# Which engine copies the transposed q and k out of PSUM in three slots of a fused attention and feed-forward kernel, and where two split products close

## The chip, the cores and the metric

The kernel runs on one core of a Trainium2 chip. A core has engines that run side by side and meet through semaphores: TensorE (matrix products and transposes, PE in the profile), VectorE (DVE), ScalarE (ACT), GpSimd (POOL) and SyncE (SP, which here only issues DMAs). Each engine takes its instructions in the order in which they were written. The metric is the device time in microseconds: a median of 348.01 us over 3 runs (348.01 to 348.04).

## The reference

Batch 8, 8 heads, sequence 576, head dimension 64; then a feed-forward layer over 4608 tokens of width 512, with 2048 hidden units.

```python
scores = scale * np.matmul(q, k.transpose(0, 1, 3, 2))
cum = np.cumsum(np.log(np.clip(f, 0.0001, 1.0)), axis=-1)
decay = cum[:, :, :, None] - cum[:, :, None, :]
scores = np.where(causal, -1000000000.0, scores + decay)
attn = np.exp(scores - np.max(scores, axis=-1, keepdims=True))
attn = attn / (np.sum(attn, axis=-1, keepdims=True) + 1e-09)
x = np.matmul(attn, v)            # heads side by side: (4608, 512)
h = x @ w_in                      # (4608, 2048)
out = (h - np.tanh(h)) @ w_out    # (4608, 512)
```

## The kernel before

Work is dealt in **slots** `p`, one for each pair of heads: slot p is batch p // 4, pair p % 4, so there are 32, and one more at the end. `NPAIR` is 4. Slot p computes the scores of its pair, the attention values of the pair before (`values`), and, early in the program, transposes q and k of a pair that comes next. Between these, a loop deals steps of the feed-forward layer, in order, so many to a slot (`TAKE`: 2 in slot 4, 7 in slot 5, 6 in each of slots 6, 7 and 8, 8 in slot 9).

**Scores.** A slot has seven tiles (`TILES`), each of up to 512 columns in one PSUM bank: `scores` (L306) issues the products K^T Q on TensorE (L326), an exp on ScalarE (L335), and, from batch 1 on, the causal mask on GpSimd (L345). The score banks are two (`ps_sc`), taken in turn, so a tile's products wait until the exp of the tile two before has read its bank. Tile 3 is the small one that both heads share.

**Transposes.** `trans` (L254) does a pair of heads' q or k for the first three batches: six transposes on TensorE (L264) into one PSUM bank, then two copies into `QT` or `KT`, one for the even and one for the odd positions (64x576 each). The letters of `copies` say which engine makes each copy: "V" is VectorE (L277), "A" is ScalarE (L275). From slot 4 on, the bank is the single one of the pool `ps_tr`. So the transposes of k wait until both copies of q have read that bank, and the next q for both copies of k. From batch 3 on, q and k are transposed by DMA and `trans` isn't used.

**Where they stand.** `att_items` (L547) writes a slot's list of items. In slots 4 to 6 the next pair's q is transposed at tile 0 and its k at tile 2 (slot 4) or 3 (slots 5, 6), with "VV". Slots 7 and 8 do two pairs of batch 2 each: q at tiles 0 and 4, k at tiles 2 and 6, with "VA" for both. There the copy on ScalarE waits for the one on VectorE.

**The feed-forward steps.** `mlp1(u, ft)` (L398) makes one 128x512 tile of h from four chunks of input (`XR`, one chunk for each pair of heads; L408), a tanh on ScalarE (L413) and an add on VectorE into `gq` (L417). Its PSUM bank comes from the three of `ps_m`, in turn; the tanh's tile `th` has two buffers. `mlp2_plain` (L436) makes a fourth of an output tile (L442) from `gq`; every fourth step ends with a copy on ScalarE (L446) and a DMA out. Slots 4 and 5 and most of slot 6 deal `mlp1` steps; slots 7 and 8 deal `mlp2_plain` steps only. The first two `mlp1` tiles are split in slot 4: three chunks first (part 0), and the last chunk with tanh and add later (part 1), since that chunk comes from the pair of the slot before, transposed and copied into `XR` by ScalarE (L378) in the same slot.

**Order.** Everything is under a manual schedule: each engine executes in the order in which the program emits. An item that counts (`put`) may be followed by a feed-forward step; one that doesn't (`items.append((fn, False))`) never moves them. The subtractions on the second layer's weights (L245) stand as such items at tiles 1, 3 and 5 of slots 7 and 8.

Of the kernel before, what the change touches and what calls it, by code (L numbers as in the profile page):

```python
# [21 lines left out]
def kernel(  # L22
# [18 lines left out]
    NPAIR = H // 2  # L41
# [39 lines left out]
    qn, kn = ([t[0:S // NT6, :].rearrange("p (h n d) -> p h n d", h=H, n=NT6) for t in raw] for raw in (qraw, kraw))  # L81
    qb, kb = ([t[:, 0:NJ * DM].rearrange("p (n e) -> p n e", n=NJ) for t in raw] for raw in (qraw, kraw))
    vn = [qkp.tile([P, NJ, H, VW], FP16, tag=f"vn{i}", name=f"vn{i}") for i in range(2)]
    QT = [qkp.tile([D + 3, H, S], FP16, tag=f"QT{i}", name=f"QT{i}") for i in range(2)]
    KT = [qkp.tile([D + 3, H, PITCH], FP16, tag=f"KT{i}", name=f"KT{i}") for i in range(2)]
# [82 lines left out]
    def load_aug(b):  # L168
        i, hs = b % 2, slice(b * H, (b + 1) * H)
        eng = nc.gpsimd if b == 0 else nc.sync  # L170
        eng.dma_start(out=KT[i][D:D + 1, :, 0:S], in_=chi[hs, :])
        eng.dma_start(out=QT[i][D + 2:D + 3, :, :], in_=cq[hs, :])
        eng.dma_start(out=KT[i][D + 1:D + 2, :, 0:S], in_=clo[hs, :])

    def const_rows(i):
        nc.sync.dma_start(out=QT[i][D:D + 2, :, :], in_=minus16)
        nc.sync.dma_start(out=KT[i][D + 2:D + 3, :, 0:S], in_=ones16[0:H, :])
# [76 lines left out]
    def trans(b, c, src, dst, early, copies, split=False):  # L254
        pn, g3 = S // NT6, NT6 // 2
        if early:
            t32 = ps_m.tile([P, UW], FP32, tag="m", name="t32")
            t16 = t32.bitcast(FP16)[:, 0:2 * S // 2].rearrange("p (a g n) -> p a g n", a=2, g=g3)
        else:
            t32 = ps_tr.tile([P, UW], FP32, tag="tr", name="t32")  # L260
            t16 = t32.bitcast(FP16)[:, 0:2 * S // 2].rearrange("p (a g n) -> p a g n", a=2, g=g3)
        for a in range(2):
            for g in range(g3):
                nc.tensor.transpose(out=t16[:, a, g, :],  # L264
                                    in_=src[b % 2][:, 2 * c + a, 2 * g:2 * g + 2, :],
                                    identity=id16[0:pn, 0:pn])
        parts = [(a, e) for a in range(2) for e in range(2)] if split else [(slice(0, 2), e) for e in range(2)]

        def copy(a, e, eng):
            if split:  # L270
                a = slice(a, a + 1)
            to = dst[b % 2][0:D, 2 * c:2 * c + 2, e:S:2].rearrange("d a (p g) -> d a p g", g=g3)[:, a]
            of = t16[e * D:(e + 1) * D, :, :, :].rearrange("d a g p -> d a p g")[:, a]
            if eng == "A":
                nc.scalar.activation(out=to, in_=of, func=AF.Copy)  # L275
            else:
                nc.vector.tensor_copy(out=to, in_=of)  # L277

        todo = [lambda a=a, e=e, eng=eng: copy(a, e, eng) for (a, e), eng in zip(parts, copies)]
        for fn in todo[:2]:  # L280
            fn()
        return todo[2:]

    def head_tiles(a):
        return [[(a, 0, 0, 512, 0)],
                [(a, 1, P, 448, 0), (a, 0, 512, 64, 448)],
                [(a, 2, 2 * P, 320, 0), (a, 3, 3 * P, 192, 320)]]

    TILES = head_tiles(0) + [[(0, 4, 512, 64, 64), (1, 4, 512, 64, 128)]] + head_tiles(1)
    LAST = 3  # L290
    MASKS = {0: (0, 1, 1, P), 1: (0, 1, 1, P), 2: (0, 2, 320, P), 3: (64, 2, 64, 64),
# [229 lines left out]
    def start():  # L521
        unread(33)
        q_rest = trans(*pairs[0], qn, QT, True, "AAAA", True)
        nc.scalar.activation(out=cq, in_=cum, func=AF.Copy, bias=-SHIFT * inv_qscale, scale=inv_qscale)
        nc.scalar.activation(out=expo, in_=lf[0:1, 0:1], func=AF.Exp)
        unread(6)
        k_rest = trans(*pairs[0], kn, KT, True, "VVVV", True)
        unread(22)
        decay(0)
        unread(8)  # L530
        scores(*pairs[0], 0)
        for fn in k_rest:
            fn()
        q_rest[0]()
        scores(*pairs[0], 1)
        q_rest[1]()
        for e in EL[0:2]:
            nc.vector.memset(e, 0.0)
        nc.vector.memset(KT[0][:, :, S:PITCH], 0.0)
# [7 lines left out]
    def att_items(p):  # L547
        def put(fn, *args):
            items.append((lambda: fn(*args), True))

        items = []
        here = pairs[p] if p < len(pairs) else None
        before = pairs[p - 1] if 0 < p <= len(pairs) else None
        after = pairs[p + 1] if p + 1 < len(pairs) else None
        early = p < NPAIR
        for ti in range(len(TILES)):
            if here and (p > 0 or ti > 1):
                put(scores, *here, ti)
            if p == 1 and ti == 6:
                items.append((lambda: const_rows(1), False))  # L560
                items.append((lambda: load_aug(1), False))
            if early and p > 0 and ti in (0, 6):
                put(unread, 2)
            if p == 1 and ti == 3:
                put(last)
            for load in LOADS.get((p, ti), ()):
                items.append((load, False))
            at_q, at_k = (1, 3) if p == 0 else (0, 1) if early else (0, 2) if p == NPAIR else (0, 3)
            if p in (2 * NPAIR - 1, 2 * NPAIR) and ti % 2 == 0:
                pair = pairs[2 * NPAIR + 2 * (p - 2 * NPAIR + 1) + ti // 4]  # L570
                put(trans, *pair, *((kn, KT) if ti % 4 else (qn, QT)), False, "VA")
            if ti == at_q and p < 2 * NPAIR - 1:
                put(trans, *after, qn, QT, early, "VV")
            if p == NPAIR:
                if ti in (3, 4):
                    put(mlp1, 0, ti - 3, 1)
            if ti == at_k and p < 2 * NPAIR - 1:
                put(trans, *after, kn, KT, early, "VV")
            if p == NPAIR:
                if ti == 1:  # L580
                    put(turn, *pairs[p - 2])
                    put(values, *before)
                    put(mlp1, 0, 0, 0)
                elif ti == 2:
                    put(mlp1, 0, 1, 0)
                    put(turn, *before)
            elif early and ti in (2, 3) and before:
                put(values, *before, (ti - 2,))
            elif not early and ti == 2 and before:
                put(values, *before)  # L590
            if p < NPAIR:
                if ti == 1 and p > 1:
                    put(turn, *pairs[p - 2])
            elif p > NPAIR and ti == 3:
                put(turn, *before)
        return items
# [9 lines left out]
    with tc.manual_schedule(engines=FIVE):  # L606
        bulk()
        for p in range(len(pairs) + 1):
            b, c = divmod(p, NPAIR)
            items = att_items(p)  # L610
            take = TAKE[p] if p < len(TAKE) else 8 - (p - len(TAKE)) % 2
            if p == 2 * NPAIR + 1:
                widen(1)
            mine = mlp[at:at + take]
            at += take
            first = 14 if p == NPAIR else 0
            if p == len(pairs):
                for fn, *args in mine[0:2]:
                    fn(*args)
                mine = mine[2:]  # L620
            given, n = 0, 0
            whole = sum(counts for _, counts in items)
            for emit, counts in items:
                emit()
                n += counts
                while n > first and given < len(mine) and given * (whole - first) < (n - first) * len(mine):
                    fn, *args = mine[given]
                    fn(*args)
                    given += 1
        widen(2)  # L630
        for fn, *args in mlp[at:]:
            fn(*args)
# [28 lines left out]
```

## Time and profile before

| | |
|---|---|
| median of 3 runs | 348.01 us |
| the profiled execution's own time | 347.95 us |
| its span | 346.2 us |
| VectorE copies of q and k, 64x576 | 0.80 us each |
| ScalarE copies of q and k, 64x576 | 0.81 us each |
| ScalarE exp of 128x512 | 0.60 us each |

The page gives busy time, share and number of instructions for each engine; a stretch gives its length, then each engine's busy time, the granted TensorE clock, the DMA engines' share and what they moved. A timeline line gives start, length, engine, line, operation and, in brackets, how long the engine had been idle and who ended that. A line of the waits gives who waited for whom, the sum, how often and the longest. TensorE's products overlap: a 128x512 product is shown 0.38 us long, but four of them take 0.86 us.

### The profile page before, as it was taken

Reading aid. Unit: us, or ns where it says so; the run is one execution under the profiler, and the core shown is the slowest. Engines: PE = TensorE matmul, PEld = TensorE weight load, DVE = VectorE, ACT = ScalarE, POOL = GpSimd, SP = SyncE. Lnnn points to the kernel's source line nnn. Section 1 sums busy time; section 2 is a strip of 40 time slices with the busy share of each in tenths; the row PEclk is TensorE's granted clock in tenths of the full one; section 3 lists DMA queues with packets and bytes.
Section 4 is the critical chain, followed back from the end, with each engine's and each line's share of the span. In section 5 each row is a group of like instructions: output and inputs, shape, how many; then the busy total and the mean of one; then the engine's idle time right before and its main releaser. Section 6 shows DMA issues by size and latency. Waiting matters only on the chain.

```text
span 346.2 us, 8606 instructions
## 1 busy us (share of the span) xinstructions
PE 335.2 (97%) x3253; PEld 230.6 (67%) x3253; DVE 261.7 (76%) x504; ACT 232.6 (67%) x437; POOL 161.3 (47%) x319
## 2 busy tenths in 40 slices
PE   8988998889999999999999999999999999999995
PEld 7476554555578656865688888755875587487485
DVE  6599787564988788678867886788677766876874
ACT  5687886777897787778767876788548842632640
POOL 8974652676558655765577465742322210000000
PEclk9999999999999999999999999999999999999999
DMA  8999999999999999799979997991131013003003
GB/s 108 147 182 201 193 201 154 107 114 177 132 130 105 177 137 122 94 176 137 117 78 200 130 128 78 186 143 27 49 97 31 17 50 110 0 14 109 0 11 113
DMA packets 144877, 38.80 MB, mean 112 GB/s; under 512 B 128148, under 2 KB 143236, under 8 KB 144836
## 3 DMA queue, kind: packets, MB, share of 16 engines
q0 software_dynamic: 92480, 18.39, 69.7%
q1 hardware_dynamic: 52356, 19.88, 30.5%
q8 instruction: 25, 0.41, 0.5%
q14 instruction: 16, 0.13, 0.1%
HBM read 36.85 MB, written 9.44 MB: 134 GB/s over the span
## 4 chain that ended last, share of the span: by engine, by line
PE 87%; DVE 6%; ACT 4%; issue 1%; DMA 1%; ACTq 0%
PE hps L408 32%; PE ops L466 28%; PE ps L326 12%; PE av L357 8%; PE ops L442 3%; DVE gq L417 2%; ACT e L335 2%; DVE QT L277 2%; PE t L264 1%; DVE KT L277 1%; PE ps L329 1%; DMA TQ<-in_f_dram 1%; PE ps L297 1%; ACT QT L275 1%; ACT th L413 1%
## 5 line engine op out<-in xcount | busy, mean ns | idle before, releaser
L408 PE MATMUL hps<-XR,win 128*128 128x512 f16 (+1 forms) x640 | 140.9, 357 | 0.9 <-ACT XR L378 0.7
L413 ACT ACTIVATE th<-hps 128x512 f32<-128x512 f32 x144 | 86.9, 603 | 55.4 <-PE hps L408 54.6
L335 ACT ACTIVATE e<-ps 128x512 f16<-128x512 f32 x192 | 110.5, 598 | 14.1 <-PE ps L326 6.0
L417 DVE TENSOR_TENSOR gq<-hps,th 128x512 f16<-128x512 f32 x144 | 98.4, 688 | 26.0 <-ACT th L413 24.6
L345 POOL TENSOR_SCALAR_AFFINE_SELECT e<-e 128x128 f16<-128x128 f16 x168 | 60.4, 361 | 78.0 <-ACT e L335 76.1
L408 PEld LDWEIGHTS <-win 128*128 128x128 f16 x640 | 57.7, 97 | 48.4 <-issue 0.5
L326 PE MATMUL ps<-QT,KT 67*128 67x64 f16 (+5 forms) x384 | 77.9, 276 | 3.1 <-ACT e L335 1.7
L466 PEld LDWEIGHTS <-gq 128*128 128x128 f16 x640 | 60.4, 97 | 11.1
L466 PE MATMUL ops<-wout,gq 128*128 128x256 f16 x512 | 63.2, 272 | 0.0
L326 PEld LDWEIGHTS <-KT 67*128 67x128 f16 (+1 forms) x384 | 36.7, 98 | 25.5 <-DVE KT L277 1.6
L357 PEld LDWEIGHTS <-e 128*128 128x128 f16 x896 | 32.2, 97 | 3.9
L357 PE MATMUL av<-vn,e 128*128 128x65 f16 x896 | 33.6, 193 | 0.0
L119 POOL DMA_DIRECT2D vn<-in_v_dram x32 | 28.0, 878 | 8.7 <-DMA win<-in_moe_w_in_dram 4.1
L466 PE MATMUL ops<-W,sq 128*128 128x256 f16 x256 | 31.2, 272 | 0.0
L366 DVE TENSOR_TENSOR xn<-av,rs 128x640 f16<-128x640 f32 x32 | 26.4, 825 | 1.1
L466 PEld LDWEIGHTS <-sq 128*128 128x128 f16 x256 | 24.2, 98 | 3.4
L96 POOL DMA_DIRECT2D kn<-in_k_dram x25 | 21.2, 848 | 1.5 <-issue 1.3
L345 POOL TENSOR_SCALAR_AFFINE_SELECT el<-el 128x128 f16<-128x128 f16 x28 | 9.4, 334 | 26.9 <-ACT el L335 26.2
L96 POOL DMA_DIRECT2D qn<-in_q_dram x25 | 21.2, 848 | 1.3 <-issue 0.8
L364 DVE TENSOR_SCALAR rs<-av 128x10 f32<-128x10 f32 x32 | 5.2, 162 | 19.0 <-PE av L357 17.9
L277 DVE COPY QT<-t 64x576 f16<-64x576 f16 x18 | 14.5, 803 | 6.2 <-PE t L264 6.1
L277 DVE COPY KT<-t 64x576 f16<-64x576 f16 (+1 forms) x22 | 16.3, 739 | 3.8 <-PE t L264 3.6
(82 smaller groups left out, 307.5 us busy)
## 6 DMA issues: line engine op xcount, KB each, us to landing
out_dram<-ost SPq DMA_DIRECT2D x34, 256.0 KB
vn<-in_v_dram POOLq DMA_DIRECT2D x24, 128.0 KB, 5.6
qn<-in_q_dram POOLq DMA_DIRECT2D x20, 128.0 KB, 4.3
kn<-in_k_dram POOLq DMA_DIRECT2D x20, 128.0 KB, 4.6
win<-in_moe_w_in_dram POOLq DMA_DIRECT2D x2, 1024.0 KB, 14.8
wout<-in_moe_w_out_dram POOLq DMA_DIRECT2D x2, 1024.0 KB, 14.1
XR<-xn SPq DMA_TRANSPOSE x56
vn<-in_v_dram POOLq DMA_DIRECT2D x12, 64.0 KB, 5.2
```

Source lines behind the costliest of these rows:

```text
L96: nc.gpsimd.dma_start(out=dst[b % 2][0:pn, n, :].rearrange("p (h d) -> p h d", h=H), in_=src[b, :, n * P:n * P + pn, :].rearrange("h p d - ...
L119: nc.gpsimd.dma_start(out=vn[b % 2][:, n, h0:h1, 0:D], in_=v[b, h0:h1, n * P:(n + 1) * P, :].rearrange("h p d -> p h d"))
L277: nc.vector.tensor_copy(out=to, in_=of)
L326: nc.tensor.matmul(out=ps[:, col:col + n], lhsT=KT[b % 2][0:rows, h, j * P:(j + 1) * P], rhs=QT[b % 2][0:rows, h, i0:i0 + n], start=not ow ...
L335: nc.scalar.activation(out=e[:, lo:hi], in_=ps[:, lo:hi], func=AF.Exp, scale=qscale)
L345: nc.gpsimd.affine_select(out=view, in_=view, compare_op=ALU.is_ge, fill=0.0, base=0, pattern=pat, channel_multiplier=-1)
L357: nc.tensor.matmul(out=av[:, a, ib, :], lhsT=E.pop((b, c, a, j, ib)), rhs=vn[b % 2][:, j, 2 * c + a, 0:D + 1], start=(j == 0), stop=(j == ib))
L366: nc.vector.tensor_tensor(out=xn.rearrange("p i (a d) -> p a i d", a=2), in0=av[:, :, :, 0:D], in1=rs.to_broadcast([P, 2, NJ, D]), op=ALU. ...
L408: nc.tensor.matmul(out=hps[:, o:o + n], lhsT=win[:, ci, ft * P:(ft + 1) * P], rhs=XR[:, ci, t:t + n], start=(ci == 0), stop=(ci == NCH - 1))
L413: nc.scalar.activation(out=th, in_=hps, func=AF.Tanh, scale=-1.0)
L417: nc.vector.tensor_tensor(out=GQ[(u, i)][:, half, kt, :], in0=hps, in1=th, op=ALU.add)
L466: nc.tensor.matmul(out=ps[:, m, :], lhsT=LHS[lhs](u, kt // 4)[:, kt % 4, m * P:(m + 1) * P], rhs=rhs[:, kt, :], start=(fresh and (apart or ...
```

## The change

In slot 6, q's two copies move from VectorE to ScalarE ("AA"); k's stay on VectorE. In slots 7 and 8, q's two copies are both ScalarE's and k's are both VectorE's ("VV"). With "AA" only the first copy is emitted right behind the transposes; the second is kept in a list and emitted at the next tile, behind that tile's exp. In slot 4 the second parts of the two split first products stand at tiles 4 and 5 instead of 3 and 4.

```diff
@@ trans @@
-        for fn in todo[:2]:
+        now = 1 if copies == "AA" else 2
+        for fn in todo[:now]:
             fn()
-        return todo[2:]
+        if copies == "AA":
+            LATER.extend(todo[now:])
+        return todo[now:]
...
+    LATER = []
+
+    def rest():
+        LATER.pop()()
@@ att_items @@
             if p in (2 * NPAIR - 1, 2 * NPAIR) and ti % 2 == 0:
                 pair = pairs[2 * NPAIR + 2 * (p - 2 * NPAIR + 1) + ti // 4]
-                put(trans, *pair, *((kn, KT) if ti % 4 else (qn, QT)), False, "VA")
+                put(trans, *pair, *((kn, KT, False, "VV") if ti % 4 else (qn, QT, False, "AA")))
+            elif p in (2 * NPAIR - 1, 2 * NPAIR) and ti % 4 == 1 or p == 2 * NPAIR - 2 and ti == 1:
+                items.append((rest, False))
             if ti == at_q and p < 2 * NPAIR - 1:
-                put(trans, *after, qn, QT, early, "VV")
+                put(trans, *after, qn, QT, early, "AA" if p == 2 * NPAIR - 2 else "VV")
             if p == NPAIR:
-                if ti in (3, 4):
-                    put(mlp1, 0, ti - 3, 1)
+                if ti in (4, 5):
+                    put(mlp1, 0, ti - 4, 1)
```

## The prediction

> **What bounds the kernel now.** I read the page's engine shares and slices first, then the busy times by stretch, the waits, the chain of waits over 53 to 68 us, and the timelines of ScalarE and TensorE through slots 4 to 9. Slots are told in the trace by their first score product, 512 columns wide. I write sc0 to sc6 for a slot's seven score tiles, M1, M2, ... for the feed-forward steps dealt between them, Q and K for six transposes of q or k.
>
> The page's engine line, and the stretches of slot 6, slot 7, slot 8 and the start of slot 9:
>
> ```profile
> PE 335.2 (97%) x3253; PEld 230.6 (67%) x3253; DVE 261.7 (76%) x504; ACT 232.6 (67%) x437; POOL 161.3 (47%) x319
> 47.50:56.60 9.10, 7.98 (x78) 4.45 (x78) 8.04 (x14) 7.18 (x14) 3.11 (x10) 1.00 1.66 186
> 56.60:66.60 10.00, 8.96 (x90) 5.19 (x91) 6.12 (x11) 6.13 (x11) 5.69 (x11) 1.00 1.63 115
> 66.60:77.10 10.50, 9.14 (x91) 5.20 (x91) 6.18 (x11) 8.01 (x14) 6.66 (x12) 1.00 1.19 109
> 77.10:90.00 12.90, 12.90 (x106) 6.88 (x106) 7.81 (x14) 10.78 (x21) 8.17 (x17) 1.00 1.65 169
> ```
>
> TensorE is the first figure after the stretch's length: full from 77.1 us on (its waits there sum to 0.2), about 1 us short in each of slots 6, 7 and 8. So whatever moves sc0 of slot 9 (77.09) moves the end one for one, at a granted clock of 1.00. The chain of waits in slots 6 and 7 shows the shortfalls:
>
> ```profile
> 55.71 0.81 DVE KT L277
> 56.52 0.05 issue
> 56.57 0.39 PE ps L326
> ...
> 57.83 0.27 PE t L264 x6
> 58.10 0.02 issue
> 58.12 0.81 DVE QT L277
> 58.93 0.02 issue
> 58.95 0.82 ACT QT L275
> 59.77 0.04 issue
> 59.82 0.41 PE t L264 x6
> ```
>
> First, slot 7's sc0 waits for slot 6's last k copy on VectorE. Then K waits for both q copies, because Q and K share one PSUM bank: Q starts at 57.66, K at 59.82, 2.16 us, with the ScalarE copy strictly behind the VectorE one. The other three gaps from Q to K are 63.85 to 66.00, 68.14 to 70.29 and 74.32 to 76.47, 2.15 each. ScalarE's own order and durations (start, length):
>
> ```profile
> 47.56 0.60 ACT L413 ACTIVATE th<-hps 128x512 f32<-128x512 f32 x1 [0.67 <-DVE gq L417]
> 48.05 1.08 ACT L335 ACTIVATE e<-ps 128x512 f16<-128x512 f32 x2
> 49.01 1.29 ACT L413 ACTIVATE th<-hps 128x512 f32<-128x512 f32 x2
> 50.20 1.08 ACT L335 ACTIVATE e<-ps 128x512 f16<-128x512 f32 x2
> 51.15 0.62 ACT L413 ACTIVATE th<-hps 128x512 f32<-128x512 f32 x1
> ...
> 58.95 0.81 ACT L275 ACTIVATE QT<-t 64x576 f16<-64x576 f16 x1 [1.29 <-DVE QT L277]
> 59.79 1.09 ACT L335 ACTIVATE e<-ps 128x512 f16<-128x512 f32 x2
> ```
>
> An exp or tanh is 0.60 long, but the next starts 0.48 after it (they overlap by 0.12); a 64x576 copy is 0.81 and the next starts 0.83 to 0.84 after it (seven cases in slots 7 and 8). The same copy on VectorE is 0.80, a pair 1.60. For slot 4, three lines of the waits:
>
> ```profile
> PE t L264 <- ACT QT L275: 1.7, 4, 0.4
> PE hps L408 <- ACT XR L378: 0.7, 1, 0.7
> PE ps L326 <- ACT e L335: 0.4, 2, 0.2
> ```
>
> **Slot 4.** Removed nothing; the fourth input chunk of M(0,0) and M(0,1), with their tanh and VectorE add, goes behind one more score tile. No DMA is issued by these steps and none is passed on SP or POOL. Now TensorE stands from 34.25 to 34.93 for the ScalarE copy into XR, with sc4 behind it, and ScalarE idles 0.30 (35.05 to 35.34) before the first tanh. After it, sc4 (0.22, its bank free at 34.00) runs in that hold and its exp takes the idle time. ScalarE then runs at its 0.48 pitch from 35.03; the first tanh comes at 35.51 instead of 35.34, but the fourth at 37.91 instead of 38.23. VectorE's add of slot 5's M1, where the chain moves onto VectorE, was at 39.89 and comes at about 39.65, since M1's last product ends 38.97. From there VectorE is on the chain up to 47.46, and hands the gain to the tanh at 47.56: -0.24. Bounds: -0.30 (all of the idle time); +0.20 if the later first add keeps M(0,3) waiting for its bank, by the one such wait shown (TensorE on the add, 0.20). If that cover failed, VectorE would start its q pair in slot 5 later.
>
> **Slot 6.** VectorE loses the q pair (50.27 to 51.90, 1.63). ScalarE gains two copies: the first behind M1's tanh, the second behind sc1's exp, so both stand ahead of M3's tanh. ScalarE's queue is in order, and from 47.56 it was nearly full: tanh, exp, exp, tanh 49.01, copy 49.50, tanh 50.33, exp 50.81, copy 51.31, exp 52.14, tanh of M3 52.62 to 53.22 (it was 51.15 to 51.77). Who waits: M3's add on VectorE, and behind it in VectorE's queue the division of the attention values, M4's add and the k pair. Before, add 52.54, first division step 53.13, k pair 54.92 to 56.52. After, the add starts 53.27, the division 53.87 (0.60 on, as in the trace), the k pair 55.66 (1.79 on), and ends 57.26; sc0 of slot 7 at 57.31 instead of 56.57: +0.74. VectorE's saved 1.63 turns into idle time before its adds. The q pair itself is done at 52.12, ahead of K at 52.63. Bounds: +0.98 if a copy doesn't overlap the exp or tanh ahead of it (the start-up copies of q show a step of 0.50 after the exp at 9.72 and 0.62 after that at 10.75; I take 0.50, as between the exp at 68.11 and the output copy at 68.61), and -1.26 if the relief arrived whole: sc6 leaves TensorE at 55.31.
>
> **Slots 7 and 8.** Each Q to K gap was 0.46 (transposes to first copy), 0.83, 0.82, 0.05. Now the two copies are on ScalarE with sc1's (or sc5's) exp between: 0.46 + 0.83 + 0.50 + 0.81 + 0.05 = 2.65, +0.49 or so each. Work between Q and K on TensorE is 1.57, so all of it is stall. In slot 8's second gap M5's output copy (0.60, started 0.20 after Q at 74.52, pitch 0.50) is ahead of the first copy: 0.70 + 2.19 = 2.87 instead of 2.15, +0.72; before, VectorE's half hid it. K to the next Q: k pair 0.46 + 1.61 + 0.05 = 2.12 against 2.14 where it bound (66.00 to 68.14): nothing; from slot 7's and slot 8's first K to Q2 TensorE's own 4.03 covers it. The division behind the k pair starts 2.2 after K, the pair ends 2.07 after it: covered by 0.1. The exp of sc5 no longer follows both copies, so sc0 of slot 9 doesn't wait for it: K to sc0 was 0.62 (76.47 to 77.09), becomes the transposes' 0.26: -0.36. The same wait at slot 8's start gives nothing, since Q behind it waits for the k pair anyway. Sum 3 x 0.49 + 0.72 - 0.36 = +1.83. Bounds: +2.31 with 0.12 more at each exp-to-copy step; +1.35 if the four first copies overlapped their exps by 0.12 as exps do; as a floor -0.72, both sc0 waits and nothing else. I take the rows of these very copies.
>
> The Trainium skill (ScalarE: Activation LUTs, What ACT_TABLE_LOAD costs) says that back-to-back ACTIVATEs overlap by about 93 ns. By it the six copies followed by an exp or tanh would cost 0.56 less, and the time would be about 349.7; the trace agrees for exps (0.12) and not for these copies.
>
> **Sum.** -0.24 + 0.74 + 1.83 = +2.33 against the profiled execution's 347.95 us (span 346.2), which is 0.06 under the median of 348.01: 350.3.
>
> **Rivals.** A, not slower: VectorE's relief reaches slot 7. The place is M3's tanh in slot 6. Ending at 51.77 as now, it would let the add start at 51.82 and the k pair end at 55.81: sc0 at 55.86, -0.71, total +0.88, 348.8; earlier still, sc0 comes at 55.31, -1.26, total -0.24 - 1.26 + 1.83 = +0.33, 348.3. It decides where that tanh ends before about 51.6 instead of 53.22: then slot 6's term is -0.87 and the sum within 0.70. For it: VectorE is the fullest engine there after TensorE (8.04 of 9.10). Against: two copies, 1.67 us, ahead of a tanh that had 0.77 of slack (its end at 51.77, its add at 52.54). B, not slower: sc1's exp doesn't separate the halves, both run back to back before it. Then the gaps are 0.46 + 0.83 + 0.81 + 0.05 = 2.15 as now, 0.20 more for the output copy, and -0.24 + 0.74 + 0.20 - 0.36 = +0.34, 348.4. For it: nothing but that order; against: in this trace every engine follows the order written. A with B: -1.66, 346.3. C, slower still: the copies don't overlap what is ahead of them: -0.24 + 0.98 + 2.31 = +3.05, 351.0, and with slot 4 at its +0.20, +3.49, 351.5. For it: the step of 0.62 at start-up; against: the 0.50 there and after other exps.
>
> **Numbers.** About 0.2% (0.70 us) is what a measurement of this kernel can tell from no change. Forecast 0.74, with its own range 349.5 (-0.30 + 0.50 + 1.35) to 351.0; C 0.10; A 0.08; B 0.04; A with B 0.04. Slower 0.84, same 0.12, faster 0.04. Low 348.9, part way to A, since slot 6 may give back some; high 351.5 from C.
>
> **What would show it.** Right: the gap from Q to K near 2.65 three times and 2.87 once; M3's tanh in slot 6 later by over 1 us and sc0 of slot 7 waiting for KT near 57.1; sc0 of slot 9 near 79.4; TensorE full after it. Slot 4: no hold for XR with sc4 behind it, and slot 5's first add 0.2 earlier. Wrong: a KT ready before slot 6's last score tile; K starting 2.2 after Q; ScalarE copies shorter than 0.8; or idle time after slot 9 that takes up the delay.

## The result, and the profile after

The changed kernel takes 350.04 us (median of 5, 350.02 to 350.9) against 348.03 (348.01 to 348.07): 2.01 us slower; over all five runs the ratio is 1.0064, 95% interval 1.0052 to 1.0075. Some runs show a granted clock of 0.993 to 0.995 and take 0.7 to 1.7 us longer (two of these five, seven of the 12 of slot 6 alone and two of the six with q in another bank, both below), and no difference told here rests on them. The forecast was 350.3, slower, in a range from 348.9 to 351.5.

The page's engine line after, and the stretches of slot 6, slot 7, slot 8 and the start of slot 9, whose bounds have moved with the slots (length, then TensorE, its weight loads, VectorE, ScalarE, GpSimd, the granted clock, DMA share, GB/s):

```profile
PE 334.9 (96%) x3253; PEld 230.0 (66%) x3253; DVE 260.2 (75%) x502; ACT 234.1 (67%) x439; POOL 162.3 (47%) x319
47.20:57.00 9.80, 8.05 (x79) 4.46 (x78) 6.59 (x12) 8.43 (x16) 3.32 (x10) 1.00 1.71 183
57.00:67.50 10.50, 8.78 (x90) 5.11 (x91) 5.25 (x9) 7.04 (x12) 6.32 (x11) 1.00 1.47 114
67.50:79.10 11.60, 9.03 (x96) 5.11 (x93) 6.20 (x10) 7.90 (x14) 7.17 (x12) 1.00 1.10 99
79.10:92.00 12.90, 12.90 (x110) 6.87 (x107) 8.79 (x15) 9.97 (x20) 7.86 (x16) 1.00 1.53 156
```

TensorE's work in the three slots is what it was, to within 0.2 us in each; the slots are longer: 9.8, 10.5 and 11.6 us against 9.1, 10.0 and 10.5. VectorE is relieved in slot 6 (6.59 us busy against 8.04) and ScalarE is loaded (8.43 against 7.18), and the slot takes longer all the same. From slot 9 on TensorE is full as before: sc0 of slot 9 starts at 79.08 instead of 77.09, and what follows takes 269.22 us instead of 269.11. So 1.99 of the 2.1 us by which the span grew lie before slot 9.

The chain of waits of the changed kernel over 50 to 62 us (start, length, what; lines behind `trans` have moved by 8, so the tanh is L421, the add L425, the scores L334):

```profile
50.97 0.73 ACT QT L275
51.70 0.12 issue
51.81 0.60 ACT e L343
52.41 0.50 ACT th L421
52.91 0.02 issue
52.94 0.69 DVE gq L425
...
56.12 0.81 DVE KT L277
56.93 0.05 issue
56.97 0.39 PE ps L334
...
58.52 0.24 ACT QT L275
58.76 0.44 issue
59.20 0.57 ACT e L343
59.77 0.03 issue
59.79 0.81 ACT QT L275
60.61 0.04 issue
60.65 0.42 PE t L264 x6
```

In slot 6 the chain now runs through ScalarE: the second q copy, an exp, M3's tanh, and only then VectorE's add and its k pair. In slot 7 an exp stands between the two q copies for which K waits. VectorE's timeline in slot 6 says the same from its side, first before, then after:

```profile
50.27 1.63 DVE L277 COPY QT<-t 64x576 f16<-64x576 f16 x2
...
54.92 1.60 DVE L277 COPY KT<-t 64x576 f16<-64x576 f16 x2
```
```profile
50.49 0.69 DVE L425 TENSOR_TENSOR gq<-hps,th 128x512 f16<-128x512 f32 x1 [0.43 <-ACT th L421]
52.94 0.69 DVE L425 TENSOR_TENSOR gq<-hps,th 128x512 f16<-128x512 f32 x1 [1.75 <-ACT th L421]
...
55.33 1.59 DVE L277 COPY KT<-t 64x576 f16<-64x576 f16 x2
```

In place of the 1.63 us that VectorE spent on q it now waits 1.75 us for a tanh. TensorE's waits over the three slots, first the one before for slot 6's k pair, then all of the changed kernel:

```profile
PE ps L326 <- DVE KT L277: 1.1, 1, 1.1
```
```profile
PE t L264 <- ACT QT L275: 3.7, 4, 1.1
PE ps L334 <- DVE KT L277: 1.7, 1, 1.7
PE t L264 <- DVE KT L277: 0.6, 1, 0.6
```

TensorE stands 3.7 us for the q copies (1.7 before), 1.7 for slot 6's k pair (1.1 before), and 0.6 where slot 8's first Q waits for a k pair (0.3 before, for the k copy on ScalarE).

### The profile page after: what moved, and what is told of

It reads as the page before. It is cut to its first block, busy times and chain, and to the rows that moved or that the text cites. A ratio compares the mean times of both kernels' runs of the same rounds, so it can differ in the third digit from the quotient of the medians.

```text
span 348.3 us, 8609 instructions
## 1 busy us (share of the span) xinstructions
PE 334.9 (96%) x3253; PEld 230.0 (66%) x3253; DVE 260.2 (75%) x502; ACT 234.1 (67%) x439; POOL 162.3 (47%) x319
## 4 chain that ended last, share of the span: by engine, by line
PE 90%; ACT 4%; DVE 3%; issue 1%; DMA 1%; ACTq 0%
PE hps L416 35%; PE ops L474 28%; PE ps L334 12%; PE av L365 8%; PE ops L450 2%; ACT e L343 2%; PE t L264 2%; ACT QT L275 2%; DVE KT L277 1%; PE ps L337 1%; DMA TQ<-in_f_dram 1%; PE ps L305 1%; PE ps L303 0%; DVE TQ L159 0%; DVE gq L425 0%
## 5 line engine op out<-in xcount | busy, mean ns | idle before, releaser
L421 ACT ACTIVATE th<-hps 128x512 f32<-128x512 f32 x144 | 86.9, 605 | 54.0 <-PE hps L416 52.3
L425 DVE TENSOR_TENSOR gq<-hps,th 128x512 f16<-128x512 f32 x144 | 98.4, 688 | 28.0 <-ACT th L421 26.6
L353 POOL TENSOR_SCALAR_AFFINE_SELECT e<-e 128x128 f16<-128x128 f16 x168 | 61.5, 368 | 76.6 <-ACT e L343 74.7
L334 PE MATMUL ps<-QT,KT 67*128 67x64 f16 (+5 forms) x384 | 77.7, 276 | 3.3 <-DVE KT L277 1.7
L334 PEld LDWEIGHTS <-KT 67*128 67x128 f16 (+1 forms) x384 | 36.6, 98 | 25.9 <-DVE KT L277 2.0
L277 DVE COPY KT<-t 64x576 f16<-64x576 f16 (+1 forms) x26 | 19.5, 749 | 11.1 <-PE t L264 10.8
L489 ACT ACTIVATE m<-ops 128x512 f32<-128x512 f32 x16 | 9.6, 597 | 10.9 <-PE ops L474 10.9
```

Source lines behind the costliest of these rows:

```text
L334: nc.tensor.matmul(out=ps[:, col:col + n], lhsT=KT[b % 2][0:rows, h, j * P:(j + 1) * P], rhs=QT[b % 2][0:rows, h, i0:i0 + n], start=not ow ...
L353: nc.gpsimd.affine_select(out=view, in_=view, compare_op=ALU.is_ge, fill=0.0, base=0, pattern=pat, channel_multiplier=-1)
L421: nc.scalar.activation(out=th, in_=hps, func=AF.Tanh, scale=-1.0)
L425: nc.vector.tensor_tensor(out=GQ[(u, i)][:, half, kt, :], in0=hps, in1=th, op=ALU.add)
```

## The experiments

All are edits of one of the two kernels or of an earlier version; the diffs show the lines that matter, and the helpers `LATER` and `rest` are those of the change. The kernel before, run beside them on the same chip, took 347.94 to 347.97 us.

**One part at a time.** The three parts of the change were put into the kernel before singly.

Slot 4 alone:

```diff
-                if ti in (3, 4):
-                    put(mlp1, 0, ti - 3, 1)
+                if ti in (4, 5):
+                    put(mlp1, 0, ti - 4, 1)
```

> The kernel before with slot 4's part of the change alone. Theory (three separate terms, each as in the prediction): 0.24 less, and the trace after suggests 0.30 (M1 of slot 6 came at 47.22 instead of 47.52): 347.7 to 347.8, with slots 6 to 8 as before but earlier. Rival (the later close makes M(0,3) wait for its bank): 0.2 more, 348.2. Rival (no share in it, what looked like slot 4's gain was something else): 348.0.

Measured 347.65 us against 347.97, 0.32 less (ratio 0.9995, interval 0.9982 to 1.0008, so by the runs alone it is not told from nothing; ten of the 12 runs lie between 347.60 and 347.70, the other two at 349.06 and 349.43). The trace is clearer: M1 of slot 6 starts at 47.20 instead of 47.52, sc0 of slot 9 at 76.75 instead of 77.09, and ScalarE goes straight on where it idled for 0.30:

```profile
34.78 0.27 ACT L335 ACTIVATE el<-ps 128x128 f16<-128x128 f32 x1
34.94 0.60 ACT L335 ACTIVATE e<-ps 128x512 f16<-128x512 f32 x1
35.42 0.62 ACT L413 ACTIVATE th<-hps 128x512 f32<-128x512 f32 x1
```

The first rival's wait is there, about 0.14 (M(0,3) starts at 36.81, just behind the first add, which ends at 36.75, where TensorE was free from 36.67), but it doesn't undo the gain; by the trace the second rival falls too.

Slot 6 alone:

```diff
+            elif p == 2 * NPAIR - 2 and ti == 1:
+                items.append((rest, False))
             if ti == at_q and p < 2 * NPAIR - 1:
-                put(trans, *after, qn, QT, early, "VV")
+                put(trans, *after, qn, QT, early, "AA" if p == 2 * NPAIR - 2 else "VV")
```

> The kernel before with slot 6's part alone (both q copies on ScalarE, the second a tile later). Theory (the copies push M3's tanh, and with it VectorE's k pair, past the start of slot 7): 0.70 to 0.74 more, 348.7, sc0 of slot 7 near 57.3, and a wait of VectorE for a tanh over 1.5 us in slot 6. Rival A (the relief of VectorE reaches slot 7): 0.7 to 1.26 less, 346.8 to 347.3.

Measured 348.74 us in the five runs at the full clock (348.72 to 348.76), 0.77 more than before; over all 12 runs, the longest of 349.94, the ratio is 1.0036 (1.0023 to 1.0049), so slower either way. In the profile the granted clock is 1.00 over the stretch that decides, 47 to 58 us: sc0 of slot 7 starts at 57.24 instead of 56.57, and VectorE's longest wait for a tanh is 1.74. That is what the theory said, and rival A falls.

Slots 7 and 8 alone:

```diff
+            elif p in (2 * NPAIR - 1, 2 * NPAIR) and ti % 4 == 1:
+                items.append((rest, False))
...
-                put(trans, *pair, *((kn, KT) if ti % 4 else (qn, QT)), False, "VA")
+                put(trans, *pair, *((kn, KT, False, "VV") if ti % 4 else (qn, QT, False, "AA")))
```

> The kernel before with the part of slots 7 and 8 alone. Theory (the exp between the halves lengthens each gap from Q to K): 1.6 (the steps that the trace after shows) to 1.83 more, 349.6 to 349.8, with gaps of 2.59 three times and 2.81 once. Rival (the loss needs slot 6's delay ahead of it, since both come from one overloaded ScalarE): well under 1 more.

Measured 349.67, 1.70 more (ratio 1.0044, 1.0027 to 1.006). The starts of K behind Q in TensorE's timeline give gaps of 2.58 (57.66 to 60.24), 2.59, 2.59 and 2.81. No delay in slot 6 is needed. The parts sum to -0.32 + 0.77 + 1.70 = +2.15 against the whole's +2.01: they are separate terms, to within 0.14.

**Is it the exp between the halves?** The changed kernel with both q copies right behind the transposes:

```diff
-        now = 1 if copies == "AA" else 2
+        now = 2
...
-        if copies == "AA":
-            LATER.extend(todo[now:])
...
-            elif p in (2 * NPAIR - 1, 2 * NPAIR) and ti % 4 == 1 or p == 2 * NPAIR - 2 and ti == 1:
-                items.append((rest, False))
```

> The changed kernel, but with both q copies emitted right behind the transposes, no exp between them. Theory (the exp between the halves is what lengthened the gaps): the gaps from Q to K go back to 2.14 three times and about 2.35 in slot 8's second (M5's output copy is still ahead); the wait of sc0 for sc5's exp comes back; slots 7 and 8 are 0.2 over the kernel before, slot 4 -0.33, slot 6 as in the change +0.75, in all +0.6, 348.6. Rival (two ScalarE copies in a row are slow by themselves): gaps of 2.5 or more and about 350.

Measured 348.54, 0.60 more than before (ratio 1.0017, 1.0006 to 1.0028). TensorE's timeline around slot 7's first gap, and ScalarE's:

```profile
58.09 0.42 PE L264 MATMUL t<-id,qn 96*128 96x96 f16 x6
...
60.22 0.41 PE L264 MATMUL t<-id,kn 96*128 96x96 f16 x6 [0.41 <-ACT QT L275]
```
```profile
58.55 1.63 ACT L275 ACTIVATE QT<-t 64x576 f16<-64x576 f16 x2 [0.47 <-PE t L264]
60.20 1.08 ACT L341 ACTIVATE e<-ps 128x512 f16<-128x512 f32 x2
```

The gap is 2.13, as with the pair split over two engines; the other gaps are 2.14, 2.14 and 2.36. sc0 of slot 7 starts at 57.00, as in the changed kernel (56.97), so slot 6's loss is still there, and the exp between the halves in slots 7 and 8 is worth 1.4 us of the change's 2.01. That ScalarE's copy waited for VectorE's in the kernel before was not time lost: two copies in a row on one engine take as long.

**Is it the shared bank?** The changed kernel, with q's transposes of slots 7 and 8 in a bank of `ps_m`, which the plain second-layer steps leave free there. `early` chooses nothing but the bank:

```diff
-                put(trans, *pair, *((kn, KT, False, "VV") if ti % 4 else (qn, QT, False, "AA")))
+                put(trans, *pair, *((kn, KT, False, "VV") if ti % 4 else (qn, QT, True, "AA")))
```

> The changed kernel, with the transposes of q in slots 7 and 8 in one of the three feed-forward banks instead of the single transpose bank, so that K doesn't wait for the q copies; every engine's order is the same. Theory (the loss in slots 7 and 8 is the shared bank): the stalls there (0.86 to 1.09 at each K, 0.62 at slot 8's Q) vanish; against the kernel before slots 7 and 8 lose all their 3.5 us of standing time, with slot 4 at -0.30 and slot 6 at +0.70, 344.7 to 345.5. Rival (ScalarE's added work is the loss, whatever the bank): 349.5 or more.

Measured 345.43 (over all six runs the ratio to the kernel before is 0.9937, 0.9914 to 0.996), 2.54 under the kernel before and so about 4.5 under the changed one, with every engine's order and work unchanged. In its profile TensorE waits once in slots 7 and 8, 0.2 us, and else goes from step to step, as here from 65 us on:

```profile
65.29 0.42 PE L264 MATMUL t<-id,qn 96*128 96x96 f16 x6
65.55 0.38 PE L334 MATMUL ps<-QT,KT 67*128 67x448 f16 x2
65.77 1.03 PE L450 MATMUL ops<-wout,gq 128*128 128x512 f16 x4
66.63 0.38 PE L334 MATMUL ps<-QT,KT 67*128 67x320 f16 x2
66.86 0.42 PE L264 MATMUL t<-id,kn 96*128 96x96 f16 x6
67.11 0.38 PE L334 MATMUL ps<-QT,KT 67*128 67x512 f16 x1
```

Q to K is 1.57 here, TensorE's own work; the version below with the same slots 7 and 8 (344.75) has 1.57, 1.57, 1.62 and 1.57 in its four gaps. So ScalarE carries the copies without harm in slots 7 and 8. What cost time was the shared bank: K couldn't start before q's copies, nor slot 8's first Q before the k pair.

**Is it M3's tanh in slot 6?** Slot 6's part alone, with both q copies behind that tanh (emitted behind the values):

```diff
-        now = 1 if copies == "AA" else 2
+        now = 0 if copies == "AA" else 2
...
-        LATER.pop()()
+        LATER.pop(0)()
...
-            elif p == 2 * NPAIR - 2 and ti == 1:
-                items.append((rest, False))
...
             elif not early and ti == 2 and before:
                 put(values, *before)
+                if p == 2 * NPAIR - 2:
+                    items.append((rest, False))
+                    items.append((rest, False))
```

> The kernel before with slot 6's q copies on ScalarE, but both behind M3's tanh (emitted behind the values). Theory (slot 6's loss is the delay of M3's tanh, and with it of VectorE's queue): against 348.74 with the copies ahead of that tanh, most of the loss goes; K then waits 0.7 for the copies, but TensorE has that much to spare in slot 6; sc0 of slot 7 near 56.5, 347.8 to 348.1. Rival (the loss is ScalarE's 1.6 us of added work wherever it stands): 348.6 or more.

Measured 347.84, 0.10 under the kernel before (ratio 0.9994, 0.9985 to 1.0003: no difference that can be told) and 0.9 under the same copies ahead of that tanh. VectorE's timeline:

```profile
51.79 0.69 DVE L425 TENSOR_TENSOR gq<-hps,th 128x512 f16<-128x512 f32 x1 [0.78 <-ACT th L421]
...
54.07 0.69 DVE L425 TENSOR_TENSOR gq<-hps,th 128x512 f16<-128x512 f32 x1 [0.41 <-ACT th L421]
54.68 1.61 DVE L277 COPY KT<-t 64x576 f16<-64x576 f16 x2
```

M3's add is at 51.79 instead of 53.19, and sc0 of slot 7 at 56.35 instead of 57.24. K waits 0.52 for the copies, and slot 6 has that to spare: sc0's wait for the k pair is 0.22, where it was 1.10 in the kernel before.

**Which half comes first.** In the changed kernel the first copy of a pair is 0.67 ahead of the next exp and the second 0.83; the prediction had 0.83 for both. The odd half was put first:

```diff
-        parts = ... else [(slice(0, 2), e) for e in range(2)]
+        parts = ... else [(slice(0, 2), e) for e in ((1, 0) if copies == "AA" else (0, 1))]
```

> The changed kernel with the odd half (input partitions 64 to 127) copied first and the even half (0 to 63) a tile later. In the change the first copy is 0.67 ahead of the next exp and the second 0.83. Theory (a ScalarE instruction that reads PSUM from another starting partition than the one before isn't started until that one has ended): the pattern changes sides: 0.83 behind the first copy and about 0.67 behind the second, 0.48 from the exp to the second copy, gaps of about 2.63; time within 0.2 of the changed kernel. Rival (it goes by place in the order): still 0.67 behind the first and 0.83 behind the second.

One run, 350.19. ScalarE in slot 7, first the changed kernel, then this one:

```profile
58.52 0.81 ACT L275 ACTIVATE QT<-t 64x576 f16<-64x576 f16 x1 [0.46 <-PE t L264]
59.20 0.57 ACT L343 ACTIVATE e<-ps 128x512 f16<-128x512 f32 x1
59.79 0.81 ACT L275 ACTIVATE QT<-t 64x576 f16<-64x576 f16 x1
60.62 0.60 ACT L343 ACTIVATE e<-ps 128x512 f16<-128x512 f32 x1
```
```profile
58.47 0.81 ACT L275 ACTIVATE QT<-t 64x576 f16<-64x576 f16 x1 [0.47 <-PE t L264]
59.30 0.60 ACT L343 ACTIVATE e<-ps 128x512 f16<-128x512 f32 x1
59.80 0.79 ACT L275 ACTIVATE QT<-t 64x576 f16<-64x576 f16 x1
60.45 0.57 ACT L343 ACTIVATE e<-ps 128x512 f16<-128x512 f32 x1
```

The pattern changes sides: 0.83 behind the odd copy wherever it stands, and 0.68 and 0.65 behind the even one; 0.59 from the exp to an odd copy and 0.50 to an even one. It goes by the half, not by the place. The gaps are 2.63, 2.63 and 2.64, and 2.99 in slot 8's second, where the odd copy now stands behind the output copy (0.62 on instead of 0.49).

**A version that beats both.** Slot 4's part, slots 7 and 8 with q in its own bank, and slot 6 as before:

```diff
-            elif p in (2 * NPAIR - 1, 2 * NPAIR) and ti % 4 == 1 or p == 2 * NPAIR - 2 and ti == 1:
+            elif p in (2 * NPAIR - 1, 2 * NPAIR) and ti % 4 == 1:
                 items.append((rest, False))
...
-                put(trans, *after, qn, QT, early, "AA" if p == 2 * NPAIR - 2 else "VV")
+                put(trans, *after, qn, QT, early, "VV")
```

> Slot 4's part of the change, slots 7 and 8 as in the change but with q's transposes in a feed-forward bank, and slot 6 as before (both q copies on VectorE). Theory (the terms are separate): the 0.75 that slot 6's part cost is taken off the version with the change in all three slots and the other bank (345.43): 344.7. Rival (with the stalls of slots 7 and 8 gone, slot 6's delay is taken up there): 345.4.

Measured 344.75 (ratio 0.9911, 0.9891 to 0.993), 0.68 under the version with slot 6's copies on ScalarE. Then slot 6's k transposes were put right behind the values:

```diff
-            if ti == at_k and p < 2 * NPAIR - 1:
+            if ti == at_k and p < 2 * NPAIR - 1 and p != 2 * NPAIR - 2:
                 put(trans, *after, kn, KT, early, "VV")
...
             elif not early and ti == 2 and before:
                 put(values, *before)
+                if p == 2 * NPAIR - 2:
+                    put(trans, *after, kn, KT, early, "VV")
```

> The last version (344.75: slot 4 as changed, slot 6's copies on VectorE, q's own bank in slots 7 and 8), with slot 6's k transposes right behind the values instead of behind the next score tile and M4. Theory (VectorE's queue ahead of the k pair sets sc0 of slot 7): the pair goes ahead of M4's add, which takes 0.60 of that queue, so 0.6 less, 344.1 to 344.2. Rival (the k transposes, now ahead of tile 3 and M4 on TensorE, or the later add, cost as much elsewhere): 344.7 or more.

Measured 344.17 (ratio 0.9886, 0.9865 to 0.9906). VectorE's k pair, and sc0 of slot 7 on TensorE:

```profile
53.97 1.60 DVE L277 COPY KT<-t 64x576 f16<-64x576 f16 x2
55.60 1.29 DVE L425 TENSOR_TENSOR gq<-hps,th 128x512 f16<-128x512 f32 x2
```
```profile
55.62 0.39 PE L334 MATMUL ps<-QT,KT 67*128 67x512 f16 x1 [0.25 <-DVE KT L277]
```

M4's add now follows the pair, and TensorE's wait for KT is 0.25.

## Why the prediction was right

**TensorE full from slot 9 on**, so that a shift of sc0 of slot 9 is the result: this held, with 1.99 us of shift against 2.1 of span.

**Slot 4**, forecast -0.24: the trace after has M1 of slot 6 0.30 earlier, the part alone gave -0.32. sc4's exp took ScalarE's idle time, as forecast, but the path behind it was another. The forecast had VectorE carry the gain, on the chain up to 47.46; in the trace after the chain lies on TensorE from 34.94 to 45.18. The tanh of slot 5's M1 (38.96) is held by M1's own products, which end at 38.93, and VectorE's adds go along, 0.30 earlier (39.59 instead of 39.89). That the gain comes out as ScalarE's whole idle time, the bound given, is luck as far as the runs show.

**Slot 6**, forecast +0.74: 0.40 later at sc0 of slot 7 with slot 4's 0.30 ahead of it, so +0.70; alone 0.67 in the trace and 0.77 in the time. The chain of who waits for whom (copies, tanh, add, division, k pair) is the one forecast, and moving the copies behind the tanh took the loss away. Rival A, the natural reading of a busy VectorE that is relieved, failed because its queue waits for ScalarE's: M3's tanh starts at 52.31, and A needed it to end before 51.6.

**Slots 7 and 8**, forecast +1.83: 1.99 - 0.40 = +1.59. The mechanism was right, since gaps of 2.59, 2.59, 2.60 and 2.81 were forecast as 2.65 and 2.87, and with the exp taken out from between the halves they fell back to 2.14 and 2.36. The mis-sized term is the pitch of the copies: 0.83 and 0.50 were taken for the first copy and the exp, and 0.67 and 0.60 were measured, 0.06 less in each of four gaps, which is the missing 0.24. The row used, of ScalarE copies in the kernel before, was of odd halves alone, and five of the six copies that the sum takes at 0.83 are even halves. The two errors go opposite ways, so it is partly luck that their sum is small: in slot 6 the same two steps are 0.66 and 0.65, and nearly cancel. Rival C's condition, no overlap with what is ahead, held for the odd halves and not for the even ones.

**Rival B's price** was wrong. With both copies ahead of the exp, the exp of sc5 follows both of them again, so sc0 of slot 9 waits for it and the -0.36 doesn't belong in B's sum. Without it B is +0.70; the kernel with B's order took 0.60 more than the one before, and in its trace sc0 waits 0.21 for that exp. Two slips changed nothing: rival A at its threshold sums to +0.72, just outside 0.70, and one of the seven steps behind a ScalarE copy is 0.85.

The sum was 0.3 too high, most of it that pitch; about 0.1 us that the span gained behind slot 9 was not forecast and isn't traced to a cause.

## What to carry to other kernels

Moving work off the busier engine gained nothing here, because that engine's queue waits, in order, for the engine that received it: look up what the receiver has next in its queue and who waits for that. Where two steps share one buffer, whatever is put between the last two readers of the first is added to the second's wait; a second buffer took about 4.5 us off the changed kernel here, three times what taking the exp out from between the copies did. And a copy moved to another engine is priced with its pitch among its neighbours, not its length.

## What was not expected of the hardware

Whether a ScalarE copy out of PSUM overlaps its neighbours depends here on which half it copies. In slots 7 and 8, a copy from partitions 64 to 127 is followed by an exp 0.83 to 0.84 us on and an exp by it 0.59 to 0.60 on, their full lengths; for one from partitions 0 to 63, of the same size and length, it is 0.65 to 0.68 and 0.49 to 0.50. For VectorE the Trainium skill (VectorE: DVE Perf Modes, Two Vector instructions with no wait between them) describes this: an instruction whose input starts at another group of 32 partitions than the last one read from the same memory starts only when the earlier ones have finished. The trace agrees on VectorE, where the two copies of a pair are 0.80 apart, the whole length of one. On ScalarE the change of sides in one run fits the same rule but doesn't show it alone: the halves also differ in the positions they write, even or odd, and no run separates the two. What speaks for the partitions read is the start-up of the kernel before, where a pair of such copies (64x288, the odd half last) runs from 5.93 to 6.93 and an instruction of ScalarE that reads SBUF starts at 6.79, before the odd copy has ended.
